# Attention, DFT mixing and feed-forward in one program: the feed-forward two slots earlier, w2's low halves on VectorE, the layer norm of even chunks in one block

## The chip, the cores and the metric

The kernel runs on one core of a Trainium2 chip. The metric is the device time of one execution in microseconds. The time before is the median of three runs. The trace is of one more execution, with the profiler on.

## What is computed

```python
# attention: local window of 32 keys each side plus 32 global tokens, 8 batches, 8 heads, 512 + 32 tokens, head 64
s_ll = where(|i - j| <= 32, q_l @ k_l.T / 8, -1e9);  s_lg = q_l @ k_g.T / 8
out_l = softmax([s_lg, s_ll]) @ [v_g; v_l];          out_g = softmax(q_g @ [k_g; k_l].T / 8) @ [v_g; v_l]
x = heads of [out_g; out_l] side by side             # (8, 544, 512)
# mixing and feed-forward
u  = x + real(fft(fft(x, axis=1), axis=2))
un = (u - mean(u)) / sqrt(var(u) + 1e-6)
y  = u + relu(un @ w_ch1) @ w_ch2                    # w_ch1 512 x 2048, w_ch2 2048 x 512
```

## The kernel before

All matrix products take fp16 operands in two parts, a high half and a low half (the value less its high half), and three matmuls for each product. So every operand is split: one copy to fp16 on ScalarE, one subtraction on GpSimd or VectorE. A DMA transpose on SyncE's queue turns what TensorE needs turned.

The work has three parts, which overlap:

- **Attention**, in slots. A batch takes 16 slots (four pairs of heads, four slots each, 128 queries a slot); six empty slots (`PAUSE`) stand after the first batch. A pair's scores go to one PSUM buffer of which there is a single copy (tag A): `scores` (L398) and the global queries' `g_scores` (L468) take turns in it. `masked` (L408, VectorE) and `exps` (L417, ScalarE) read the scores; `g_max` (L474 to L476, VectorE) and `g_exp` (L481, L482, ScalarE) read the global ones and so release the buffer for the next `scores`. `norm` is L457 to L459, `g_norm` L511 to L513, `scales` L315 to L332 (VectorE).
- **The DFT** of a batch, 8 to 21 slots after the batch's last slot R. `d_load` (R+8), `d_tail` on VectorE (L643 to L648, R+9.8), `d_even` on VectorE (L597, L599, R+10.4), `d_odd` on GpSimd (L593), then first and second products (L677, L707, from R+14), whose results are put together by `d_as` (L714, ScalarE) and `d_df` (L723, L724, VectorE) and added to x by `d_add` (L731, L732 on GpSimd, L733, L734 on VectorE) at R+17.6, R+18.6 and R+19.6. From the second batch on, the DFT's products use one PSUM bank, `bk1`.
- **The feed-forward**, in chunks of 256 rows, 17 of them: two for each batch, and one for the rest rows of all batches. A chunk has 16 steps, eight times a first product (`f_first`, L811, 24 matmuls), `f_hi` (L816, ScalarE), `f_lo` (L820, VectorE), and a second product (`f_second`, L830, 12 matmuls). `f_end` (L835) adds the result to u.

Ahead of a chunk stands its layer norm: `l_stats` (L760 to L763 on VectorE, L764 to L767 on GpSimd), and for each of two halves `l_un` (L774, L775, ScalarE), `l_lo` (L779, VectorE) and `l_turn` (L785, a transpose). `l_root` (GpSimd) is needed at the chunk's end only. The buffer `un` exists once, so the second `l_un` waits for the first `l_lo`. In `d_tail` the tile `st` has the same tag, so the same buffer.

The order on every engine is written by hand: `run` gives each call a time, and a sort by it makes one program order. Attention and DFT are given in slots (`add`), feed-forward and layer norm in steps (`at`). `warp` lays the slots onto the steps: up to `F0` = 37 they are the same, then 23 slots (16 + `PAUSE` + `LAG`) take the 32 steps of the first two chunks, and from then on each slot takes two steps. Engines run their own queue in order, as soon as what they wait for is there.

`w2` is split in `w_split(1, f)`, f = 0 to 15, one a slot from slot 33.75: `w_hi` (L252, ScalarE), a second ScalarE pass that scales the source in place (L261), a GpSimd subtraction (L262). `w1` is split the same way, but scaled by GpSimd (L259).

```python
        for c in range(17):
            F = F0 + 16 * c
            if c == 0:
                L, x, y, z = F - 4, (.50, .60), (.02, .06), (.30, .50)
            else:
                L, x, y, z = F - 6, (1.425, 2.425), (.335, .365), (.605, .605)
```

Of the kernel before, what the change touches and what calls it, by code (L numbers as in the profile page):

```python
# [8 lines left out]
F32 = mybir.dt.float32  # L9
# [4 lines left out]
AF = mybir.ActivationFunctionType  # L14
ALU = mybir.AluOpType
# [12 lines left out]
NVB = 2  # L28
NKB = 2
W0 = -8  # L30
F0 = 37
PAUSE = 6
LAG = 1
RS0 = 1.829591166069289e-20


# [39 lines left out]
class Plan:  # L76
# [3 lines left out]
    def add(self, slot, rank, fn, *a):  # L80
        self.at(self.warp(slot + rank), fn, *a)

    def at(self, time, fn, *a):
        self.q.append((time, len(self.q), fn, a))
# [6 lines left out]
class Kern:  # L91
# [163 lines left out]
    def w_split(self, k, i):  # L255
        nc = self.nc
        f, s, w = self.w_hi(k, i)
        if k == 0:
            nc.gpsimd.tensor_mul(f, f, s.to_broadcast([P, 512]))  # L259
        else:  # L260
            nc.scalar.activation(f, f, AF.Copy, scale=s)  # L261
        nc.gpsimd.tensor_sub(w[:, 1], f, w[:, 0])  # L262

    def b_load(self, b):
# [372 lines left out]

    def d_tail(self, b):
        ve, d = self.nc.vector, self.D[b]
        st = self.p1.tile([32, 256], F32, name="st", tag="un")  # L640
        et = d["et"] = self.p1.tile([32, 513], F32, name="et")
        xt = d["xt"]
        ve.tensor_sub(st[:, 1:256], xt[:, 1:256], xt[:, 511:256:-1])  # L643
        ve.tensor_add(xt[:, 1:256], xt[:, 1:256], xt[:, 511:256:-1])
        ve.tensor_add(et[:, 0:129], xt[:, 0:129], xt[:, 256:127:-1])
        ve.tensor_sub(et[:, 129:257], xt[:, 0:128], xt[:, 256:128:-1])
        ve.tensor_sub(et[:, 257:385], st[:, 1:129], st[:, 255:127:-1])
        ve.tensor_add(et[:, 385:513], st[:, 1:129], st[:, 255:127:-1])  # L648
# [197 lines left out]
    def run(self):  # L846
        self.h = {}
        late = F0 + 16 + PAUSE + LAG

        def warp(t):  # L850
            if t < F0:
                return t
            return F0 + 32 * (t - F0) / (16 + PAUSE + LAG) if t < late else F0 + 32 + 2 * (t - late)

        plan = Plan(warp)
        add, at = plan.add, plan.at
# [3 lines left out]
        for n in range(32):  # L860
            k, t = divmod(n, 16)
            i = t if k else 4 * (t % 4) + t // 4
            s = W0 + (n if k == 0 else 16 + 3 * t // 2)
# [3 lines left out]
            if n % 4 == 3 and k == 0:  # L867
                c = n // 4
# [6 lines left out]
        add(s + 1, .62, self.w_fold)  # L875
        add(s + 2, .62, self.w_scale, 1, 0)
        for f in range(16):
            add(s + 3 + f, .75, self.w_split, 1, f)
        add(8, .09, self.load_consts)

        for b in range(B):
# [49 lines left out]
        for b in range(B):  # L931
# [32 lines left out]
            add(t + 2, .07, self.d_rest, b)  # L964
        at(F0 + 32 * 7 + 4.5, self.l_load)
        for c in range(17):
            F = F0 + 16 * c
            if c == 0:
                L, x, y, z = F - 4, (.50, .60), (.02, .06), (.30, .50)
            else:  # L970
                L, x, y, z = F - 6, (1.425, 2.425), (.335, .365), (.605, .605)
            at(L + .42, self.l_stats, c)
            for j in range(2):
                at(L + x[j], self.l_un, c, j)
                at(L + x[j] + y[1], self.l_lo, c, j)
                at(L + x[j] + z[j], self.l_turn, c, j)
            at(L + 3.43, self.l_root, c)
            for fp in range(8):
                t = F + 2 * fp
                at(t + .30, self.f_first, c, fp)  # L980
                at(t + .97, self.f_hi, c, fp)
                at(t + 1.20, self.f_lo, c, fp)
                at(t + 3.30, self.f_second, c, fp)
            for j in range(2):
                at(F + 17.82, self.f_end, c, j)
            at(F + 18.04, self.f_out, c)
# [52 lines left out]
```

## Time and profile before

| what | us |
|---|---|
| median of 3 runs (1155.44 to 1157.02) | 1156.88 |
| the profiled execution's own time | 1152.42 |
| its span, first to last instruction | 1150.5 |
| TensorE busy | 962.0 |
| VectorE, ScalarE, GpSimd busy | 708.7, 633.6, 575.1 |
| first feed-forward matmul starts at | 220.4 |

The profile's page has the busy time of each engine, the span in 40 slices of 28.8 us, and the costliest groups. TensorE fills from the first feed-forward matmul on; ahead of it, the three other engines are the busy ones. All times in the rows are from the span's start.

### The profile page before, as it was taken

How to read it: one execution, taken by the hardware profiler on the slowest of the kernel's cores; microseconds unless marked ns; L12 is line 12 of the kernel's file. 1: busy time of each engine (PE TensorE's matmuls, PEld its weight loads, DVE VectorE, ACT ScalarE, POOL GpSimd, SP SyncE). 2: the span in 40 equal slices, each digit the busy share in tenths (PEclk: the TensorE clock that was granted, in tenths of full speed). 3: DMA queues.
4: the chain of work that ended last, by engine and by line, in shares of the span. 5: the costliest groups of instructions: out<-in, count | busy, mean ns of one | idle time of the engine just before them, and what ended most of it. 6: DMA issues, size and time to landing. Idle time of an engine off the chain costs nothing.

```text
span 1150.5 us, 25346 instructions
## 1 busy us (share of the span) xinstructions
PE 962.0 (84%) x9831; PEld 682.0 (59%) x9831; DVE 708.7 (62%) x1868; ACT 633.6 (55%) x1366; POOL 575.1 (50%) x728
## 2 busy tenths in 40 slices
PE   0244226588799899999999999999999999999996
PEld 0133215465576677676766676767677666666664
DVE  6997798547866865686568656866584444413211
ACT  5768558888676656665666566656564213212210
POOL 3789375778656554665465546654573312201100
PEclk9996557699899999999999999999999999999999
DMA  7578966567387465747465746573646212011100
GB/s 267 151 152 225 276 157 141 112 135 170 75 179 151 108 167 91 141 115 165 93 138 118 170 88 143 112 179 72 135 79 130 60 58 65 24 46 38 19 19 19
DMA packets 249569, 137.63 MB, mean 120 GB/s; under 512 B 200576, under 2 KB 223200, under 8 KB 249448
## 3 DMA queue, kind: packets, MB, share of 16 engines
q1 hardware_dynamic: 249448, 136.01, 51.2%
q8 instruction: 77, 1.26, 0.5%
q14 instruction: 44, 0.36, 0.1%
HBM read 65.10 MB, written 18.35 MB: 73 GB/s over the span
## 4 chain that ended last, share of the span: by engine, by line
PE 55%; DVE 24%; ACT 8%; DMA 6%; POOL 4%; issue 2%; SPq 0%; DVEq 0%; POOLq 0%; ACTq 0%
PE ps L811 22%; PE acc L830 22%; PE S L398 2%; DMA xt<-xs 2%; ACT pe L417 2%; DVE pe L408 2%; DMA qk<-in_qk 2%; PE bk L707 2%; DVE h L820 1%; PE S L468 1%; DVE ps L195 1%; DVE ps L196 1%; DVE z L328 1%; DVE wm L197 1%; DVE ps L194 1%
## 5 line engine op out<-in xcount | busy, mean ns | idle before, releaser
L811 PE MATMUL ps<-uh,wh 128*128 128x256 f16 x3264 | 383.4, 275 | 0.0
L830 PE MATMUL acc<-wh,h 128*128 128x512 f16 x1632 | 377.3, 381 | 4.1 <-DVE u L835 2.9
L811 PEld LDWEIGHTS <-wh 128*128 128x128 f16 x3264 | 319.2, 99 | 59.4 <-issue 0.7
L830 PEld LDWEIGHTS <-h 128*128 128x128 f16 x1632 | 153.5, 99 | 174.1 <-issue 9.2
L820 DVE SCALAR_TENSOR_TENSOR h<-ps,h 128x512 f16<-128x512 f32 x136 | 93.3, 686 | 188.6 <-ACT h L816 188.0
L425 POOL TENSOR_TENSOR ph<-pe,ph 128x448 f16<-128x448 f32 x128 | 137.2, 1072 | 143.0 <-ACT ph L421 88.5
L816 ACT ACTIVATE h<-ps 128x512 f16<-128x512 f32 x136 | 80.2, 589 | 223.4 <-PE ps L811 223.3
L417 ACT ACTIVATE pe<-pe,nm 128x224 f32<-128x224 f32 x256 | 102.0, 469 | 72.1 <-DVE nm L408 71.8
L408 DVE CUSTOM_DVE_ANT_0 pe<-S,msk,z 128x224 f32<-128x224 f32 x256 | 99.6, 445 | 7.5 <-PE S L398 3.6
L446 PE MATMUL bk<-vN,pl 128*128 128x65 f16 x768 | 72.9, 203 | 31.9 <-DMA pl<-ph 10.0
L398 PE MATMUL S<-kT,qT 64*128 64x192 f16 x768 | 55.7, 269 | 44.1 <-ACT pg L482 37.5
L398 PEld LDWEIGHTS <-qT 64*128 64x128 f16 x1536 | 53.7, 101 | 49.7 <-issue 38.9
L446 PEld LDWEIGHTS <-pl 128*128 128x128 f16 x768 | 62.2, 104 | 23.9 <-DMA pl<-ph 18.4
L421 ACT ACTIVATE ph<-pe 128x448 f16<-128x448 f32 x128 | 72.0, 562 | 0.0
L448 PEld LDWEIGHTS <-pl 96*128 96x128 f16 x768 | 60.1, 104 | 17.3 <-issue 10.5
L764 POOL TENSOR_SCALAR ve<-ve 128x2 f32<-128x2 f32 x17 | 5.8, 339 | 113.3 <-DVE ve L763 113.1
L376 POOL TENSOR_TENSOR kT<-qk,kT 128x512 f16<-128x512 f32 x32 | 40.7, 1272 | 36.4 <-ACT kT L371 33.0
L723 DVE SCALAR_TENSOR_TENSOR asm<-bk,dsc,asm 128x258 f32<-128x258 f32 (+1 forms) x21 | 10.1, 482 | 75.1 <-PE bk L707 60.5
L448 PE MATMUL bk<-vB,pl 96*128 96x65 f16 x576 | 55.2, 204 | 0.0
L774 ACT ACTIVATE un<-u,ve 128x512 f32<-128x512 f32 x34 | 27.6, 811 | 47.7 <-DVE unh L779 37.7
L361 ACT ACTIVATE qk<-qk,z 128x512 f32<-128x512 f32 x64 | 45.2, 708 | 10.7 <-DVE z L326 10.7
L262 POOL TENSOR_TENSOR wh<-wm,wh 128x512 f16<-128x512 f32 x32 | 38.0, 1188 | 19.7 <-ACT wm L261 18.3
(188 smaller groups left out, 1654.8 us busy)
## 6 DMA issues: line engine op xcount, KB each, us to landing
qk<-in_qk SPq DMA_DIRECT2D x32, 512.0 KB
vf<-in_v SPq DMA_DIRECT2D x32, 320.0 KB
raw<-in_moe_w_ch SPq DMA_DIRECT2D x18, 512.0 KB
xs<-x SPq DMA_DIRECT2D x32, 256.0 KB
out<-u SPq DMA_DIRECT2D x16, 512.0 KB
rw<-in_moe_w_ch SPq DMA_DIRECT2D x12, 512.0 KB
x<-xs SPq DMA_DIRECT2D x24, 256.0 KB
u<-xs SPq DMA_DIRECT2D x24, 256.0 KB
```

The lines of the kernel that those rows point to most:

```text
L361: self.nc.scalar.activation(s[nm], s[nm], AF.Copy, scale=s["z"][:, 3:4] if nm == "q" else s["z"][:, 4:5])
L398: nc.tensor.matmul(ps, qT[r, a, j], k, start=m == 0, stop=m == 2)
L408: nc.vector.tensor_tensor_reduce(self.per[(4 * p + j) % 4][:, h, 0:224], S[:, h, 224 * n:224 * n + 224], self.msk[:, j], z[:, 8:9], 3e38, ...
L417: nc.scalar.activation(pe[:, h, 0:224], pe[:, h, 0:224], AF.Exp, bias=nm[:, n, h:h + 1], scale=-1.0)
L421: self.nc.scalar.activation(ph[:, 0, :, 0:224], self.per[i % 4][:, :, 0:224], AF.Copy)
L425: self.nc.gpsimd.tensor_sub(ph[:, 1, :, 0:224], self.per[i % 4][:, :, 0:224], ph[:, 0, :, 0:224])
L446: nc.tensor.matmul(pv[:, j % 2, h], pl[:, 4 * a + 2 * h], vN[:, j, c, h, :], start=m == 0, stop=False)
L448: nc.tensor.matmul(pv[:, j % 2, h], pl[0:96, 4 * a + 2 * h + 1], vb, start=False, stop=m == 2)
L811: nc.tensor.matmul(ps[:, q], wt[:, w, c0:c0 + P], uh[:, :, 4 * a + kt, :], start=n == 0, stop=n == 11)
L816: self.nc.scalar.activation(h[:, 0], self.fps, AF.Relu)
L820: self.nc.vector.scalar_tensor_tensor(h[:, 1], self.fps, 0.0, h[:, 0], op0=ALU.max, op1=ALU.subtract)
L830: nc.tensor.matmul(self.acc_f[j], h[:, a, q, j * P:(j + 1) * P], self.w[1, f][:, w, :], start=f == 0 and a == 0 and w == 0, stop=f == 15 a ...
```

## The change

- `F0` is 35 instead of 37, and `LAG` 0 instead of 1: the feed-forward stands two slots earlier, and 22 slots instead of 23 lie over the first two chunks. After these the attention of a given slot stands beside steps that are six later (three slots) than before.
- `w_split` for w2: one VectorE instruction makes the low half from the unscaled source. The second ScalarE pass and the GpSimd subtraction go. The splits are given in steps, not slots, so they come one each step.
- `st` in `d_tail` has a buffer of its own.
- Layer norm: for the first chunk it begins 2.8 steps ahead instead of 4. For the even chunks 2 to 14, which are a batch's first, it begins 3.9 steps ahead instead of 6, and both halves follow each other directly. Odd chunks and the last are as they were in steps.

```diff
-F0 = 37
+F0 = 35
-LAG = 1
+LAG = 0
-            nc.scalar.activation(f, f, AF.Copy, scale=s)
+            nc.vector.scalar_tensor_tensor(w[:, 1], f, s, w[:, 0], op0=ALU.mult, op1=ALU.subtract)
+            return
         nc.gpsimd.tensor_sub(w[:, 1], f, w[:, 0])
-        st = self.p1.tile([32, 256], F32, name="st", tag="un")
+        st = self.p1.tile([32, 256], F32, name="st")
-            add(s + 3 + f, .75, self.w_split, 1, f)
+            at(s + 3 + f + .75, self.w_split, 1, f)
             if c == 0:
-                L, x, y, z = F - 4, (.50, .60), (.02, .06), (.30, .50)
+                L, x, y, z = F - 2.82, (.44, .50), (.02, .06), (.20, .30)
+            elif c % 2 == 0 and c < 16:
+                L, x, y, z = F - 3.9, (.50, .60), (.02, .06), (.30, .50)
```

Lines behind the added ones move by one: L643 of before is L644 of the change, and so on.

**VectorE, the tail of the fourth batch's DFT** (slots 79 and 80). `st`, `xt`, `et` are `d_tail`, `x_6575` is `d_even`, `h` is `f_lo`, `ng` is `g_max`. Before:

```order
L643 TENSOR_TENSOR st<-xt 32x255
L644 TENSOR_TENSOR xt<-xt 32x255
L645 TENSOR_TENSOR et<-xt 32x129
L646 TENSOR_TENSOR et<-xt 32x128
L647 TENSOR_TENSOR et<-st 32x128
L648 TENSOR_TENSOR et<-st 32x128
L597 TENSOR_TENSOR x_6575<-x_6575 128x4x255
L599 TENSOR_TENSOR x_6575<-x_6575 128x2x257
L820 SCALAR_TENSOR_TENSOR h<-ps_6794,h 128x512
L474 TENSOR_REDUCE ng<-S 64x1
```

And with the change:

```order
L645 TENSOR_TENSOR xt<-xt 32x255
L646 TENSOR_TENSOR et<-xt 32x129
L647 TENSOR_TENSOR et<-xt 32x128
L648 TENSOR_TENSOR et<-st 32x128
L649 TENSOR_TENSOR et<-st 32x128
L780 TENSOR_TENSOR unh<-un,unh 128x512 x2
L598 TENSOR_TENSOR x_6681<-x_6681 128x4x255
L600 TENSOR_TENSOR x_6681<-x_6681 128x2x257
L821 SCALAR_TENSOR_TENSOR h<-ps_6918,h 128x512
L475 TENSOR_REDUCE ng<-S 64x1
```

Both `l_lo` of the odd chunk 5 now stand between `d_tail` and `d_even`; before they stood two and a half slots later, behind `scales`.

**VectorE, the end of the third batch's DFT** (slot 71). `asm` and `u` are `d_df` and `d_add`, `nm` is the end of `masked`. Before:

```order
L408 ISA nm 128x1
L723 SCALAR_TENSOR_TENSOR asm<-bk_128,dsc,asm 128x2x129
L724 SCALAR_TENSOR_TENSOR asm<-bk_128,dsc,asm 128x2x129
L733 TENSOR_TENSOR u<-u,asm 128x257
L734 TENSOR_TENSOR u<-u,asm 128x255
L820 SCALAR_TENSOR_TENSOR h<-ps_5917,h 128x512
```

With the change:

```order
L409 ISA nm 128x1
L761 BN_STATS bst<-u 128x6
L762 BN_AGGR mv<-bst 128x2
L761 BN_STATS bst<-u 128x6
L762 BN_AGGR mv<-bst 128x2
L763 TENSOR_SCALAR ve<-mv 128x2
L764 TENSOR_SCALAR ve<-ve 128x2
L780 TENSOR_TENSOR unh<-un,unh 128x512 x2
L724 SCALAR_TENSOR_TENSOR asm<-bk_128,dsc,asm 128x2x129
L725 SCALAR_TENSOR_TENSOR asm<-bk_128,dsc,asm 128x2x129
```

The whole layer norm of the even chunk 4 now stands ahead of `d_df`, which empties `bk1`; before it stood two slots later, around `scales`.

**VectorE, ahead of the first feed-forward product** (slot 32). `wsc` is w2's scale, `dn` is the first row of `norm`. Before:

```order
L734 TENSOR_TENSOR u<-u,asm 128x255
L232 TENSOR_SCALAR wsc<-bk_128 128x1
L233 RECIPROCAL wsc<-wsc 128x1
L234 TENSOR_SCALAR wsc<-wsc 128x1
L236 TENSOR_SCALAR wsc<-wsc 128x4
L237 TENSOR_SCALAR wsc<-wsc 128x1
L457 TENSOR_SCALAR dn<-bk_127,z 128x4
```

With the change:

```order
L735 TENSOR_TENSOR u<-u,asm 128x255
L761 BN_STATS bst<-u 128x6
L762 BN_AGGR mv<-bst 128x2
L761 BN_STATS bst<-u 128x6
L762 BN_AGGR mv<-bst 128x2
L763 TENSOR_SCALAR ve<-mv 128x2
L764 TENSOR_SCALAR ve<-ve 128x2
L232 TENSOR_SCALAR wsc<-bk_128 128x1
L233 RECIPROCAL wsc<-wsc 128x1
```

The six statistics rows, which stood behind this slot's `norm` and `masked`, now follow `d_add` at once.

## Rows read from the trace of the kernel before

**Rows 1.** The page: busy tenths in 40 slices, and the clock.

```profile
PE   0244226588799899999999999999999999999996
PEclk9996557699899999999999999999999999999999
```

**Rows 2.** Windows: length, busy (instructions) of PE, PEld, DVE, ACT, POOL; clock, DMA.

```profile
209.40:220.40 11.00, 3.66 (x43) 2.65 (x44) 5.74 (x20) 9.55 (x21) 8.23 (x9) 0.50 0.98 200
220.40:291.90 71.50, 58.65 (x682) 42.29 (x680) 45.43 (x124) 62.09 (x133) 58.35 (x73) 0.93 0.60 133
291.90:360.00 68.10, 63.45 (x737) 45.31 (x735) 49.46 (x140) 49.54 (x112) 44.46 (x56) 0.98 0.61 123
476.50:591.70 115.20, 111.52 (x1193) 78.98 (x1192) 76.82 (x205) 71.31 (x160) 64.94 (x82) 0.99 0.57 131
```

**Rows 3.** Timeline: start, duration, engine, line, instruction [idle before <-releaser]; the start.

```profile
208.58 0.21 PE L446 MATMUL bk<-vN,pl 128*128 128x65 f16 x1 [2.73 <-DVE xg L513]
213.49 0.64 PE L468 MATMUL S<-kT,gT 128*64 128x512 f16 x1 [4.09 <-DVE nm L408]
220.37 1.89 PE L811 MATMUL ps<-uh,wh 128*128 128x256 f16 x8
```

**Rows 4.** Timeline: the DFT's add and the first chunk's layer norm.

```profile
196.96 0.74 POOL L732 TENSOR_TENSOR u<-u,asm 128x255 f32<-128x255 f32 x1
...
203.09 0.81 ACT L774 ACTIVATE un<-u,ve 128x512 f32<-128x512 f32 x1 [2.76 <-POOL ve L767]
```

**Rows 5.** Groups by line and shape: count, busy us, mean ns, idle before.

```profile
L774 ACT ACTIVATE un<-u,ve 128x512 f32<-128x512 f32 x34 | 27.6, 811 | 47.7 <-DVE unh L779 37.7 <-POOL ve L767 9.8
L775 ACT ACTIVATE unh<-un 128x512 f16<-128x512 f32 x34 | 21.4, 630 | 1.1
L261 ACT ACTIVATE wm<-wm,wsc 128x512 f32<-128x512 f32 x16 | 11.6, 722 | 0.5
L262 POOL TENSOR_TENSOR wh<-wm,wh 128x512 f16<-128x512 f32 x32 | 38.0, 1188 | 19.7 <-ACT wm L261 18.3
L636 DVE SCALAR_TENSOR_TENSOR eh<-s,dsc,eh 128x512 f16<-128x512 f32 x8 | 6.7, 840 | 0.0
```

**Rows 6.** Timeline: TensorE's waits around the second chunk, by three releasers.

```profile
307.23 1.02 PE L830 MATMUL acc<-wh,h 128*128 128x512 f16 x4 [2.86 <-DVE u L835]
352.00 0.19 PE L446 MATMUL bk<-vN,pl 128*128 128x65 f16 x1 [1.43 <-DVE xg L513]
```

**Rows 7.** Timeline: DVE, ACT and PE at the fourth batch's `d_tail`.

```profile
495.92 2.38 DVE L643 TENSOR_TENSOR st<-xt 32x255 f32<-32x255 f32 x1
504.43 0.26 DVE L476 TENSOR_SCALAR ng<-ng,z 64x1 f32<-64x1 f32 x1
505.82 0.42 PE L398 MATMUL S<-kT,qT 64*128 64x192 f16 x6 [0.28 <-ACT pg L482]
622.36 0.42 PE L398 MATMUL S<-kT,qT 64*128 64x192 f16 x6 [1.61 <-ACT pg L482]
```

**Rows 8.** Timeline: the third batch's second products at slot 71.

```profile
443.77 0.49 DVE L723 SCALAR_TENSOR_TENSOR asm<-bk,dsc,asm 128x258 f32<-128x258 f32 x1 [2.43 <-ACT qk L361]
447.52 0.34 PE L707 MATMUL bk<-c2r,z 128*18 128x129 f16 x3
```

**Rows 9.** Timeline: TensorE's waits beside layer norms and `scales`, and VectorE's longest of these.

```profile
465.88 0.19 PE L446 MATMUL bk<-vN,pl 128*128 128x65 f16 x1 [1.37 <-DVE xg L513]
526.93 0.34 PE L677 MATMUL bk<-c1r,eh 128*128 128x137 f16 x3 [2.03 <-DVE x L459]
756.33 0.34 PE L677 MATMUL bk<-c1r,eh 128*128 128x137 f16 x3 [1.94 <-DVE x L459]
809.37 0.19 PE L446 MATMUL bk<-vN,pl 128*128 128x65 f16 x1 [1.25 <-DVE xg L513]
462.42 2.13 DVE L328 SCALAR_TENSOR_TENSOR z<-z 128x2 f32<-128x2 f32 x1
```

**Rows 10.** One line's instructions: ns min/median/max; `scales` on VectorE.

```profile
L328 DVE SCALAR_TENSOR_TENSOR z<-z x16: 162/948/2131, 22.6 to 806.0; 128x2 f32<-128x2 f32 x16
```

## The prediction

> **What bounds the kernel now.** I read the slices of the page first. The reader is to see two regimes: up to the eighth slice TensorE is mostly idle and at varying clock, and from then on it is at 80 to 100% and, but for a few slices, at full clock [rows 1]. The windows say how full it is: in the first chunk TensorE is busy 58.65 of 71.50 us, in the second 63.45 of 68.10, in a later pair of chunks 111.52 of 115.20 [rows 2]. So from 220.4 us on the end is set by TensorE's work plus its idle time. All matmuls stay, at about the same clock, so the sum needs two things: when the first feed-forward matmul can start (and what attention work it pushes behind itself), and which of TensorE's waits go or come. In the first chunk ScalarE is as full as TensorE (62.09 of 71.50), GpSimd nearly (58.35), VectorE is not (45.43) [rows 2]. That matters for the w2 edit.
>
> **A, the start.** Of before, TensorE's last `values` ahead of slot 35.3, where the first product now stands, began at 208.58 and was done by about 209.4; then it sat idle 4.09 us up to 213.49. The first product came at 220.37 [rows 3]. From 209.4 to 220.4 TensorE was busy 3.66 of 11.00 us [rows 2]. That attention work now comes behind or between, so the most that can be won is 11.0 - 3.7 = 7.3 us. Against it stands the first chunk's layer norm, which moves up to right behind `d_add`. Its second statistics instruction reads what GpSimd's L732 leaves, at 196.96 + 0.74 = 197.7 [rows 4], while VectorE gets there at about 195.4; so VectorE waits 1.5 us or more there, and behind it wait this slot's scale, `norm` and `masked`. ScalarE's first L774, which was done after a wait of 2.76 us at 203.09 [rows 4], now waits from about 195.4 to about 200, and the second one waits for a `l_lo` that stands behind `masked`. This slot's `exps`, ahead of the layer norm before, stand behind it. Following both queues, the next slots come 3 to 5 us later and the first product at about 212, not 209.4. I take -(220.4 - 212) + 3.7 = **-4.7 us**; bounds -7.3 (the layer norm costs nothing) and 0 (the lateness passes on whole).
>
> **B, the first two chunks.** The w2 edit takes 722 ns from ScalarE and 1188 ns from GpSimd for each split, and gives VectorE one instruction of a form that is there already: L636, 128x512 from fp32 with a scalar, 840 ns [rows 5]. Fourteen splits stand behind slot 35, twelve of before behind slot 37. So ScalarE loses 12 x 0.72 = 8.6 us of the first chunk's work and VectorE gets 14 x 0.84 = 11.8 us: VectorE goes from 64% to 80% of the stretch, ScalarE from 87% to 75%. The low half moreover waits, in VectorE's queue, for ScalarE's high half, with `masked` and `f_lo` behind it; before, GpSimd did the waiting. I take nothing for the edit, bounds -8.6 and +11.8. Three waits of TensorE I count. The wait of 2.86 us for `f_end` (L835) goes [rows 6], since `f_end` no longer stands behind `scales`; but now it stands behind `d_tail`, and I give half back: -2.9 + 1.5. The wait of 1.43 us beside chunk 2's layer norm [rows 6] goes: -1.4. And chunk 2's new layer norm stands on ScalarE ahead of `d_as`, with its second half behind a `l_lo` that stands behind `masked`: on the two engines some 9.5 us of work lie between two of the DFT's products, under which TensorE has 5: +4.5 (bounds 0 and +4.5). Together **+1.7 us**.
>
> **C, odd chunks from the third batch on.** Between `d_tail` and `d_even` VectorE now has both `l_lo`. The first releases `un`, ScalarE then does L774 and L775 (0.81 + 0.63 us [rows 5]), and only then can the second go, so VectorE's chain grows by 0.69 + 1.44 + 0.69 = 2.8 us (0.69 is the usual `l_lo`). In the fourth batch that chain has no gap: it begins with L643 at 495.92, ends with `g_max` at 504.43, `g_exp` follows, and TensorE's `scores`, which need the PSUM buffer, wait at 505.82 already (0.28 us), in the fifth batch 1.61 us [rows 7]. What is late there is late on TensorE. Four batches (third to sixth) have next to no slack at this place: 4 x 2.8 - 0.3 = +10.9. The seventh has about 2.7 us of slack, the eighth no attention beside it: nothing. In exchange the waits at the old place go, where the layer norm and `scales` fell together: 2.03 us at 526.93 and two like it (the last 1.94 at 756.33 [rows 9]), with what hangs on them 6.0. **+4.9 us**; bounds -6 (the new place is covered) and +11 (the old waits stay, with `scales` alone).
>
> **D, even chunks.** At slot 71 the whole block stands ahead of `d_df`, which empties `bk1`. Of before, VectorE idled 2.43 us up to 443.77 and then did `d_df`; TensorE used the bank again at 447.52 [rows 8], about 2.9 us after it was free. The statistics (2.1 us) fit into that idle time. Then come 0.9 us on GpSimd, 1.4 on ScalarE, 0.7 on VectorE, 1.4, 0.7: `d_df` is done at about 449.5 instead of 444.7, and TensorE waits 2.0 us. Four batches: +8.0. The old waits beside even layer norms go, 1.37 us at 465.88 and three like it (the last 1.25 at 809.37 [rows 9]): -5.4. **+2.6 us**; bounds -5.4 and +8.
>
> **Nothing** for `st`'s own buffer (the same six instructions; it only keeps `l_un` from waiting for `d_tail`), for `l_root` (12 short GpSimd instructions, needed at the chunk's end) and for the later DFT of the last batch: it ends in chunk 14, and its layer norm begins some 13 us of TensorE work ahead of its product, for about 12 us of chain.
>
> **What the skill says.** VectorE's `scales` on 128x2 take 162 ns at best and 2131 at worst [rows 9, 10], the worst while GpSimd works. The Trainium skill (SBUF — State Buffer, section "SBUF: two separate sides") says that VectorE and GpSimd share a port pair as an exclusive lock, taken also by a VectorE instruction with two SBUF inputs against a GpSimd instruction that reads SBUF. The trace agrees with a wait of that kind. It speaks against this edit, since the new w2 instruction has two such inputs: by it each of the 14 could wait for a GpSimd instruction of some 1.2 us, 16.8 us in all, where L636's mean is only 0.1 us above its usual duration.
>
> **Sum.** Made against the profiled execution: 1152.4 - 4.7 + 1.7 + 4.9 + 2.6 = 1156.9, that is +4.5 us. The median of the runs is 4.5 us above that execution (1156.88 against 1152.42), so for the median I predict **1161.4**.
>
> **The rivals.** *ScalarE was the bound of the first chunk, and its relief shortens the slots* (faster). For it: 62.09 of 71.50 busy. Against: TensorE is as full, and VectorE takes over more than ScalarE gives. 12 x 0.72 = 8.6 off: 1152.8. It decides the sign if more than about half of it arrives. *The new stalls of C and D don't come*, since VectorE gets to these places earlier than I think (faster): 1161.4 - 10.9 - 8.0 = 1142.5. Against it: no gap on VectorE from L643 to `g_max`. *VectorE becomes the first chunk's bound* (slower): the splits wait on ScalarE and on GpSimd, 11.8 us on the path: 1173.2. For it: `masked` and `f_lo`, on which TensorE waits, stand in the same queue; against: 45.43 busy of 71.50 leaves room. *The change doesn't do what it says*: the early start is eaten by the early layer norm, A is 0: 1166.1.
>
> **How the numbers follow.** Forecast 0.42, first rival 0.22, second 0.13, third 0.15, fourth 0.08. The forecast's own spread is 1156 to 1167 (A and D at their ends). The range of 8 in 10 reaches from 1149 to 1172: it holds the first and fourth rival and most of the third, and leaves out the second and the far part of the third. 0.2% is 2.3 us, about what a measurement tells from no change. Faster: the second rival, two thirds of the first, a little of the forecast: 0.33. Same: a third of the first, a quarter of the forecast: 0.18. Slower: the rest, 0.49.
>
> **What would show it.** The first L811 at about 212 us (A). The pair of the first two chunks about as long as before, 71.5 + 68.1 = 139.6 us [rows 2], less the work of one slot that went over to later (B). TensorE waits of about 3 us before L398 (one line later) once a batch, released by `g_exp`, from the third batch on (C), and of 2 us before L707, released by `d_df` (D); none left beside `scales`. The forecast is wrong if the later pairs of chunks keep their 115.2 us or fall below, or if the first pair falls by more than 8 us.

## The result, and the profile after the change

| | us |
|---|---|
| before, median of 7 runs (1153.98 to 1159.13) | 1157.02 |
| after, median of 7 runs (1160.45 to 1163.49) | 1161.94 |
| ratio after to before, 95% interval | 1.0050 (1.0034 to 1.0066) |
| the profiled execution of after, and its span | 1161.94, 1160.2 |
| TensorE, VectorE, ScalarE, GpSimd busy | 969.0, 685.1, 623.7, 555.0 |
| first feed-forward product starts at | 209.4 |

The change makes the kernel 0.5% slower. The profiled execution of before was one of its quickest (1152.42 us; over all measurements its runs lie between 1151 and 1161), so the two traces differ by 9.7 us where the medians differ by 4.9. Differences below that come from traces are read with this in mind; those between runs are ratios to runs of before on the same chip, turned into us with 1157.

**Where the traces part.** The windows of after, in the columns of [rows 2]: first chunk, second chunk, and the pair of the fifth and sixth.

```profile
209.40:276.20 66.80, 58.28 (x650) 41.24 (x643) 49.08 (x141) 53.74 (x119) 45.08 (x62) 0.92 0.64 128
276.20:355.10 78.90, 64.93 (x732) 45.74 (x725) 51.66 (x131) 47.95 (x108) 40.58 (x40) 0.91 0.61 135
...
472.20:587.90 115.70, 111.55 (x1193) 79.22 (x1192) 70.03 (x207) 71.63 (x159) 64.10 (x83) 0.99 0.58 129
```

The reader is to see the lengths: the first chunk takes 66.8 us instead of 71.5, the second 78.9 instead of 68.1, a later pair 115.7 instead of 115.2 [rows 2]. Chunk 2 begins at 355.1 instead of 360.0. So the trace of after is 4.9 us ahead there, and from there to the end it needs 805.1 us where before needed 790.5. Of these 14.6 us, 5.7 are TensorE's waits. The view of TensorE's waits (releaser: us in total, times, longest) from chunk 2 on, first before, then after:

```profile
PE S L398 <- ACT pg L482: 5.5, 3, 3.6
PE bk L446 <- DVE xg L513: 5.4, 4, 1.4
PE bk L677 <- DVE x L459: 5.1, 3, 2.0
PE S L468 <- DVE nm L408: 0.9, 2, 0.4
```

```profile
PE bk L708 <- DVE asm L725: 12.6, 6, 2.3
PE acc L831 <- DVE u L836: 7.7, 4, 1.9
PE bk L447 <- DVE xg L514: 2.1, 3, 1.6
PE S L399 <- ACT pg L483: 0.2, 1, 0.2
```

The two lists have almost nothing in common: 16.9 us of old waits went (L398's are those of [rows 7], L446's and L677's those of [rows 9]), 22.6 us of others came. The rest, 8.8 us, is TensorE being busy longer: three more slots of attention stand behind chunk 2, and there are five stretches of 3.4 us at a granted clock of 1.2 GHz, each right behind a wait, against two before (the last microseconds, at 1.2 GHz in both, left out).

Most of the 14.6 us falls late. The windows of chunks 10 to 13 in the columns of [rows 2], first before, then after:

```profile
819.70:923.90 104.20, 104.20 (x1091) 73.89 (x1090) 58.67 (x157) 46.30 (x96) 48.03 (x65) 1.00 0.46 97
923.90:1013.30 89.40, 89.40 (x659) 60.93 (x657) 38.79 (x75) 21.31 (x36) 20.12 (x42) 1.00 0.18 50
```

```profile
816.80:928.10 111.30, 108.55 (x1135) 76.79 (x1134) 62.62 (x184) 53.85 (x112) 55.45 (x71) 0.98 0.46 97
928.10:1022.90 94.80, 92.52 (x712) 63.20 (x711) 38.62 (x83) 22.37 (x40) 19.81 (x41) 0.98 0.19 51
```

These four chunks take 206.1 us instead of 193.6, 12.5 more. Before, TensorE was busy there without a gap; now it has two waits for `d_df`, a stretch at 1.2 GHz behind each, and the attention of the three slots. Chunks 2 to 9 together take only 461.7 us instead of 459.7, since the new waits there stand in place of old ones.

**The first `L708` wait of the list (step D).** Timeline of VectorE and TensorE at the fourth batch's slot 87:

```profile
577.01 0.69 DVE L780 TENSOR_TENSOR unh<-un,unh 128x512 f16<-128x512 f32 x1 [1.55 <-ACT unh L776]
577.62 0.48 DVE L724 SCALAR_TENSOR_TENSOR asm<-bk,dsc,asm 128x258 f32<-128x258 f32 x1
...
578.55 0.33 PE L708 MATMUL bk<-c2r,z 128*18 128x129 f16 x3 [2.00 <-DVE asm L725]
```

VectorE waits 1.55 us for the second half's `un`, does `l_lo`, and only then `d_df`, for which TensorE waits 2.00 us.

**The `L831` waits.** Timeline of VectorE at the end of chunk 4, `f_lo`, `scales` (L316 to L333), `g_norm`, then `f_end`; and TensorE's wait:

```profile
530.13 0.69 DVE L821 SCALAR_TENSOR_TENSOR h<-ps,h 128x512 f16<-128x512 f32 x1
530.74 0.15 DVE L316 TENSOR_SCALAR z<-bk 128x6 int32<-128x6 int32 x1
...
531.73 1.24 DVE L319 TENSOR_SCALAR z<-z 128x4 int32<-128x4 int32 x1
533.00 1.14 DVE L329 SCALAR_TENSOR_TENSOR z<-z 128x2 f32<-128x2 f32 x1
534.06 1.07 DVE L330 TENSOR_SCALAR z<-z,ge 128x2 f32<-128x2 f32 x1
...
536.21 1.39 DVE L836 SCALAR_TENSOR_TENSOR u<-acc,ve,u 128x512 f32<-128x512 f32 x2
```

```profile
536.99 2.75 PE L831 MATMUL acc<-wh,h 128*128 128x512 f16 x12 [1.92 <-DVE u L836]
```

`scales` takes from 530.74 to 535.7, in instructions like the one of [rows 10] that can take 0.16 us; GpSimd works beside it without a gap from 530.65 to 535.1. In after it stands at the end of every chunk, right ahead of `f_end`; in before it stood six steps earlier. TensorE waits for `f_end` from 535.1 to 537.0. The four waits are those at the ends of chunks 2, 4, 6 and 8.

**The tail of the DFT (step C).** Timeline of after at the place of [rows 7], with GpSimd's `d_odd` (L594), and then the same in before (L593, and two of VectorE's):

```profile
508.76 2.35 POOL L594 TENSOR_TENSOR s<-x 128x1020 f32<-128x1020 f32 x1
...
511.56 0.41 DVE L644 TENSOR_TENSOR st<-xt 32x255 f32<-32x255 f32 x1
...
515.48 0.69 DVE L780 TENSOR_TENSOR unh<-un,unh 128x512 f16<-128x512 f32 x1 [1.55 <-ACT unh L776]
...
518.55 0.67 DVE L475 TENSOR_REDUCE ng<-S 64x1 f32<-64x512 f32 x1
```

```profile
495.68 2.34 POOL L593 TENSOR_TENSOR s<-x 128x1020 f32<-128x1020 f32 x1 [6.32 <-DMA x<-xs]
...
498.34 1.14 DVE L644 TENSOR_TENSOR xt<-xt 32x255 f32<-32x255 f32 x1
...
501.56 1.54 DVE L599 TENSOR_TENSOR x<-x 128x514 f32<-128x514 f32 x1
...
503.62 0.67 DVE L474 TENSOR_REDUCE ng<-S 64x1 f32<-64x512 f32 x1
```

Both `l_lo` are in the chain, with the idle 1.55 us that was forecast. Yet from `d_tail`'s first instruction to `g_max`'s first it takes 7.0 us, and before, with neither of them, 7.7 (495.92 [rows 7] to 503.62). Three of the chain's instructions took 2.38, 1.14 and 1.54 us in before and take 0.41, 0.41 and 0.70 in after, 3.5 us less: in before GpSimd's `d_odd` and what follows it ran beside them, in after `d_odd` is done when `d_tail` begins. 7.7 - 3.5 + 2.8 = 7.0. It is so in the other batches too: L643 takes 2.35, 2.38 and 2.35 us in the third to fifth batch of before, and its like L644 takes 0.40 to 0.41 us in the third to eighth of after.

**The start (step A).** Timeline of after, TensorE and VectorE:

```profile
209.45 3.28 PE L812 MATMUL ps<-uh,wh 128*128 128x256 f16 x24
...
219.13 0.64 PE L469 MATMUL S<-kT,gT 128*64 128x512 f16 x1 [4.38 <-DVE nm L409]
```

```profile
208.52 2.72 DVE L330 TENSOR_SCALAR z<-z,ge 128x2 f32<-128x2 f32 x1
```

The first product came 11.0 us earlier, and then the second only at 220.68: VectorE stood in `scales` (one instruction 2.72 us), then came a w2 split and `d_df` of the last tile, with `masked` behind them, and TensorE waited 4.38 us for that. Where before it waited ahead of the first product ([rows 3]: 4.09 us), it now waits behind it.

### The profile page after: what moved, and what is told of

It is laid out like the page before. It is cut to its first block, busy times and chain, and to the rows that moved or that the text cites. A ratio compares the mean times of both kernels' runs of the same rounds, so it can differ in the third digit from the quotient of the medians.

```text
span 1160.2 us, 25359 instructions
## 1 busy us (share of the span) xinstructions
PE 969.0 (84%) x9831; PEld 686.0 (59%) x9831; DVE 685.1 (59%) x1884; ACT 623.7 (54%) x1350; POOL 555.0 (48%) x712
## 4 chain that ended last, share of the span: by engine, by line
PE 54%; DVE 25%; ACT 8%; POOL 5%; issue 4%; DMA 3%; SPq 0%; DVEq 0%; POOLq 0%
PE ps L812 23%; PE acc L831 22%; DVE pe L409 2%; PE S L399 2%; DVE h L821 2%; ACT un L775 2%; DVE ps L195 1%; DVE ps L194 1%; ACT pe L418 1%; DVE ps L196 1%; PE bk L708 1%; PE bk L678 1%; DVE wm L197 1%; PE bk L447 1%; PE S L469 1%
## 5 line engine op out<-in xcount | busy, mean ns | idle before, releaser
L831 PE MATMUL acc<-wh,h 128*128 128x512 f16 x1632 | 378.2, 382 | 13.6 <-DVE u L836 13.6
L812 PE MATMUL ps<-uh,wh 128*128 128x256 f16 x3264 | 389.3, 277 | 0.0
L812 PEld LDWEIGHTS <-wh 128*128 128x128 f16 x3264 | 322.5, 100 | 63.0 <-issue 1.2
L831 PEld LDWEIGHTS <-h 128*128 128x128 f16 x1632 | 153.7, 99 | 184.6 <-issue 20.1
L449 PEld LDWEIGHTS <-pl 96*128 96x128 f16 x768 | 59.8, 104 | 12.5 <-DMA qk<-in_qk 5.3
L377 POOL TENSOR_TENSOR kT<-qk,kT 128x512 f16<-128x512 f32 x32 | 37.7, 1178 | 42.6 <-ACT kT L372 29.6
L780 DVE TENSOR_TENSOR unh<-un,unh 128x512 f16<-128x512 f32 x34 | 24.4, 719 | 41.4 <-ACT unh L776 41.4
L698 DVE SCALAR_TENSOR_TENSOR z<-bk,z 128x274 f16<-128x274 f32 x28 | 13.2, 472 | 58.3 <-ACT z L687 58.3
L732 POOL TENSOR_TENSOR u<-u,asm 128x257 f32<-128x257 f32 x16 | 13.3, 830 | 70.0 <-DVE asm L725 65.6
```

Of the source, the lines that this page charges most:

```text
L449: nc.tensor.matmul(pv[:, j % 2, h], pl[0:96, 4 * a + 2 * h + 1], vb, start=False, stop=m == 2)
L812: nc.tensor.matmul(ps[:, q], wt[:, w, c0:c0 + P], uh[:, :, 4 * a + kt, :], start=n == 0, stop=n == 11)
L831: nc.tensor.matmul(self.acc_f[j], h[:, a, q, j * P:(j + 1) * P], self.w[1, f][:, w, :], start=f == 0 and a == 0 and w == 0, stop=f == 15 a ...
```

## The experiments

All are the changed kernel, or the kernel before, with one edit. The number in brackets is the 95% interval of the ratio to before; after the change it is 1.0050.

**1. `even`: the even chunks' layer norm taken apart about `d_df`.** The seven numbers are steps from the chunk's start: statistics, then `l_un`, `l_lo`, `l_turn` of each half. `d_df` is at -2.88; without the edit all but the last turn stand ahead of it.

```diff
+SPLIT.update({c: (-3.48, -3.40, -2.87, -2.50, -2.865, -2.62, -2.30) for c in range(4, 16, 2)})
```

> The changed kernel with the layer norm of the even chunks 4 to 14 taken apart: statistics and the first L775/L776 stay ahead of d_df, both l_lo and the second L775/L776 go behind it. Theory (step D of the prediction, as the changed kernel's trace shows it): the whole layer norm ahead of d_df is what makes TensorE wait six times 2.0 to 2.3 us ahead of L708, and four of these waits are followed by 3.4 us at the granted clock of 1.2 GHz, some 1.7 us each. Without them: 6 x 2.1 + 4 x 1.7 = 19 us off, 1143; the lines that answer to the waits at 462.5, 576.6, 691.8, 807.1, 917.3 and 1012.5 are gone, and so are the low-clock stretches behind four of them. Rival (the wait only moves): TensorE waits as long, now for g_max behind the moved l_lo or for the first product of the next chunk: 1160 to 1164.

Measured: 1146.39 us, 0.9936 (0.9924 to 0.9948), 13.2 us less than after. TensorE's waits from chunk 2 on:

```profile
PE acc L833 <- DVE u L838: 7.7, 4, 1.9
PE bk L449 <- DVE xg L516: 4.6, 5, 1.6
```

All six waits for `d_df` are gone and no stretch at 1.2 GHz is left between 372 and 1139 us. The forecast was 19; some 2.5 us came back as waits for `g_norm` (2.1 to 4.6 us), and the traces differ by 15.5. D's mechanism is shown, and the rival, that the wait only moves, is out.

**2. `scales`: `scales` behind `f_end`.**

```diff
-                add(G - 5, .62, self.scales, p // 2)
+                add(G - 5, .92 if G > 61 else .62, self.scales, p // 2)
```

> The changed kernel with scales (from the third chunk on) put behind f_end instead of ahead of it. Theory: the changed LAG put scales, whose 128x2 instructions take 1.1 to 1.2 us each beside GpSimd, right ahead of f_end, and this is the wait of 1.9 us ahead of L831 in every even chunk's end (four of them). Without it 4 x 1.9 = 7.6 us off: 1154. Rival: f_end is late for d_lo and d_tail_lo ahead of it, or scales, now later, delays the next L362 and with it the attention: under 2 us off, 1160 to 1163.

Measured: 1151.74 us, 0.9967 (0.9953 to 0.9982), 9.6 us less than after. In the same view:

```profile
PE bk L708 <- DVE asm L725: 12.5, 6, 2.3
PE bk L244 <- DVE xg L514: 1.9, 4, 0.5
```

The four waits for `f_end` are gone, and so is the 1.6 us beside `g_norm`. So `scales` ahead of `f_end` cost them, not `d_lo` or `d_tail_lo`.

**3. `both`: the two edits together.**

> The changed kernel with both edits that gained, the even layer norms taken apart about d_df and scales behind f_end. The two remove different waits in different chunks. Theory: the gains add, 13.2 + 9.6 = 22.8 us off the changed kernel's 1161.9: 1139, ratio to before 0.985. Rival (with one wait gone the other's neighbour becomes late): less than 17 us, 1145 and up.

Measured: 1134.19 us, 0.9819 (0.9798 to 0.9839), 26.7 us less than after: the gains add (22.8 us by the two alone, a difference at the edge of the intervals). From chunk 2 on TensorE waits 2.1 us in all, and the trace needs 776.3 us there instead of 805.1. That fall of 28.8 us is what the list and the clock say: 20.5 us of waits and five stretches of 3.4 us at half the clock, 8.5 us. From chunk 2 on the cause is therefore shown: beside the attention that came there, the change lost by two things, the layer norm ahead of `d_df` and `scales` ahead of `f_end`, and by what they did to the clock.

**4. and 5. The second chunk's two long waits, one at a time.** `ln2` moves chunk 2's `l_un` behind `d_as` and its second `l_lo` behind `d_df`; `tail` moves the second batch's `d_tail` behind `f_end`.

```diff
+SPLIT[2] = (-3.38, -3.02, -2.795, -2.65, -2.75, -2.07, -1.95)
```

```diff
-            add(R + 9, .80, self.d_tail, b)
+            add(R + 9, 1.265 if b == 1 else .80, self.d_tail, b)
```

> The changed kernel with chunk 2's layer norm alone taken apart: L775/L776 behind d_as, the second l_lo behind d_df. Theory (step B, its third wait): the wait of 6.07 us ahead of L708 at 337.6 is chunk 2's layer norm ahead of d_as, with its second half behind masked. Without it 6.1 us and about 2 us of low clock behind it go: 1154 to 1156. Rival: the first two chunks are bound by another engine's work, so that TensorE waits elsewhere instead: 1160 to 1163.

> The changed kernel with the second batch's d_tail put behind f_end of the first chunk. Theory: the wait of 5.93 us ahead of L831 at 286.7 is f_end behind d_tail, which first waits for its DMA (2.18 us) and then runs beside GpSimd (L644 2.11 us where it takes 0.41 alone). Without it 5.9 us and some 2 us of low clock go: 1154 to 1156. Rival: d_tail, now later, delays d_even and g_max behind it, and TensorE waits there: 1160 to 1163.

Measured: `ln2` 1159.30 us, 1.0041 (1.0029 to 1.0053), within its interval of after; `tail` 1160.06 us, 1.0053 (1.0041 to 1.0064), no change. Both rivals hold. The timeline of TensorE shows where the wait went, first in `ln2`, where L710 is the changed kernel's L708 and L717 `d_as` of the last tile, then in `tail`, where L483 is `g_exp`:

```profile
349.54 0.81 PE L710 MATMUL bk<-c2r,z 128*18 128x129 f16 x6 [4.53 <-ACT asm L717]
```

```profile
297.39 0.66 PE L399 MATMUL S<-kT,qT 64*128 64x192 f16 x6 [5.50 <-ACT pg L483]
```

In `tail` the moved `d_tail` takes as long as it did (L644 2.24 us, beside GpSimd), now ahead of `g_max`.

**6. and 7. `all2` and `best`: these two moved further.** In `all2` `d_tail` goes behind `g_max` (1.695 for 1.265), and chunk 2's layer norm wholly behind `d_df`; in `best` its first `l_un` goes forward to where ScalarE is free. Both keep the two edits of `both`.

```diff
-SPLIT[2] = (-2.075, -1.565, -1.235, -1.02, -1.025, -0.795, -0.60)
+SPLIT[2] = (-3.38, -2.59, -2.075, -1.9, -1.565, -1.5, -1.46)
```

> As the run before it, and chunk 2's layer norm wholly behind d_df (first L775 behind the last d_as, second behind f_hi), and the second batch's d_tail behind g_max of its slot. Theory: the two waits of 6.07 and 5.93 us in the second chunk only moved in the last two experiments because what was moved stood ahead of another operation TensorE waits for (the last d_as; g_exp); behind those, both go, some 10 us with their stretches at 1.2 GHz: 1129. Rival: the first two chunks are bound by VectorE's and ScalarE's chains, and the waits move once more: 1137 to 1140.

> As all2, with chunk 2's layer norm earlier: statistics behind masked, first L775 behind p_hi, first l_lo behind d_df, second L775 behind the last d_as. Theory: the 5.48 us that TensorE waited ahead of chunk 2's first product in all2 were its late second DMA transpose, and go, with some 2 us at 1.2 GHz; nothing waits in exchange, since ScalarE's queue is never held ahead of d_as: 1125 to 1128. Rival: ScalarE held by the second L775, or VectorE by l_lo ahead of g_max, gives the wait back: 1131 to 1134.

Measured: `all2` 1132.50 us, 0.9804 (0.9783 to 0.9825); `best` 1129.12 us, 0.9765 (0.9738 to 0.9792). `all2` lies between its theory and its rival, `best` 1 us above its theory. `all2` won less than 2 us on `both`: its first pair of chunks fell from 146.6 to 142.0 us, but TensorE then waited 5.48 us for chunk 2's transposes, too late now. In `best` that wait is gone, and a wait of 3.01 us for the last `d_as` came. What still bounds the first two chunks there stays open. So `best` is 27 us faster than before and 33 faster than after, and in its later pairs TensorE is busy for 109.75 of 110.40 us:

```profile
351.00:461.40 110.40, 109.75 (x1192) 78.19 (x1193) 68.08 (x208) 71.23 (x159) 64.96 (x83) 1.00 0.60 136
```

**8. `w2old`: the changed kernel without the w2 edit.**

```diff
-            nc.vector.scalar_tensor_tensor(w[:, 1], f, s, w[:, 0], op0=ALU.mult, op1=ALU.subtract)
-            return
+            nc.scalar.activation(f, f, AF.Copy, scale=s)
```

> The changed kernel with w2's low halves made as before, by a second ScalarE pass and a GpSimd subtraction. Theory (step B): the edit is worth nothing, 1160 to 1164, the first product and the first two chunks' 66.8 and 78.9 us as they are. First rival (ScalarE was the bound): 14 splits x 0.72 us come back on ScalarE, the first chunk 5 to 9 us longer, 1167 to 1171. Third rival (VectorE's new 14 x 0.84 us are on the path): the first chunk shorter, 1150 to 1156.

Measured: 1172.62 us, 1.0157 (1.0138 to 1.0177), 12.4 us more than after (10.7 by the medians alone). The first rival holds: the first chunk takes 76.1 us, as against 66.8, the pair 157.5 as against 145.7. The timeline of `w2old`, TensorE and ScalarE:

```profile
248.89 0.66 PE L398 MATMUL S<-kT,qT 64*128 64x192 f16 x6 [3.70 <-ACT pg L482]
```

```profile
244.20 0.72 ACT L261 ACTIVATE wm<-wm,wsc 128x512 f32<-128x512 f32 x1
...
247.34 0.58 ACT L816 ACTIVATE h<-ps 128x512 f16<-128x512 f32 x1
247.81 0.76 ACT L481 ACTIVATE pg<-S,ng,z 64x512 f32<-64x512 f32 x1
```

ScalarE works without a gap from 237.6 on, `g_exp` stands at its end, and TensorE waits 3.70 us for it; `g_max` had been done at 243.2. In the first chunk TensorE's waits for `g_exp` come to 6.4 us, in after to 1.6: that is 4.8 of the 9.3 us. TensorE is also busy 3.2 us longer there, at a mean clock of 0.86 against 0.92.

**9. `w2before`: the kernel before with the w2 edit alone.** The diff is that of experiment 8, the other way round.

> The kernel before with the w2 edit alone. Theory (from undoing the edit in the changed kernel, which cost 10.7 us): ScalarE's second pass bounds the first chunk in the kernel before as well (62.09 of 71.50 us busy), so the first pair of chunks gets 8 to 11 us shorter: 1145 to 1149, ratio 0.99 to 0.993. Rival: with the start at slot 37 twelve splits stand behind it and only some of them late, TensorE waits for w2 but 0.9 us there; 1153 to 1157.

Measured: 1148.94 us, 0.9935 (0.9911 to 0.9959), 7.5 us less than before. By time it is the theory. But its profiled execution, 1152.82 us, was its slowest, no shorter than the one of before, and shows only 2.3 us in the first pair of chunks (137.3), so where the 7.5 us come from is not shown.

**10. and 11. `start` and `startw2`: the early start alone, without and with the w2 edit.** The first chunk's layer norm and the splits move with it as in the change. `LAG` 3 puts chunk 2 and all behind it against the same slots as before.

```diff
-F0 = 37
+F0 = 35
-LAG = 1
+LAG = 3
-            add(s + 3 + f, .75, self.w_split, 1, f)
+            at(s + 3 + f + .75, self.w_split, 1, f)
-                L, x, y, z = F - 4, (.50, .60), (.02, .06), (.30, .50)
+                L, x, y, z = F - 2.82, (.44, .50), (.02, .06), (.20, .30)
```

> The kernel before with the early start alone: F0 = 35 with LAG = 3, so that from chunk 2 on every operation stands against the attention as before, the first chunk's layer norm behind d_add as in the changed kernel, and w2's splits timed by the feed-forward's own steps as there, but made as before. Theory (step A): the first product at about 209 to 210 us, 11 us earlier, the two first chunks longer by two slots of attention work, some 7.3 us (3.66 us each by the prediction's window): -3.7, 1151 to 1153, ratio 0.9965. Rival (the early layer norm and the denser w2 splits eat it): within 2 us of before.

> The early start alone (F0 = 35, LAG = 3, the run before) with the w2 edit. Theory: the first two chunks advance by the attention's slots, about 6.1 us each whatever feed-forward lies beside them, so an early start gives nothing by itself and its cost (9.3 us) stays: with the edit some 10 us less than the early start alone, 1153 to 1156, and slower than the edit alone. Rival (the early start only lost because ScalarE was full): with the edit it pays the 3.7 us forecast for it, 1142 to 1145 if the edit alone gives 1147.

Measured: `start` 1164.86 us, 1.0090 (1.0070 to 1.0109); `startw2` 1165.45 us, 1.0064 (1.0039 to 1.0089). The early start costs 10 us without the edit, and 15 with it (against `w2before`); for `startw2` neither the theory nor the rival came. (The expectation of `start` counts 3.66 us for each of two slots; the window of [rows 2] has 3.66 for both together.) The first product came at 209.5, and chunk 2, which begins in the same slot as before, at 370.0 instead of 360.0. The waits of `start` in its first pair of chunks:

```profile
PE S L398 <- ACT pg L482: 6.2, 4, 3.7
PE S L468 <- DVE nm L408: 4.8, 2, 4.4
PE bk L446 <- DVE xg L513: 4.8, 2, 3.4
PE ps L811 <- DMA uh<-unh: 4.4, 1, 4.4
PE acc L830 <- DVE h L820: 2.7, 1, 2.7
```

These are many waits, for VectorE, for ScalarE and for a transfer, and no one of them is as long as the loss. From the first product to chunk 2 `start` takes 160.5 us; before took 150.6 for the same slots, from 209.4 on. TensorE idles 4.2 us more in it, and is busy 5.7 us longer. Per slot the pair takes 6.4 us (160.5 for 25 slots), before 6.1 (139.6 for 23), after 6.6 (145.7 for 22), `w2old` 7.2. That a slot of attention has a length of its own here, whatever feed-forward lies beside it, as the theory of `startw2` has it, is not shown by these. Which wait of `start` carries the 10 us, and why the edit gains nothing on top of it (160.4 against 160.5 us in the traces), stays open.

**12. `oddlate`: `d_odd` behind `p_lo`.**

```diff
-            add(R + 10, .355, self.d_odd, b)
+            add(R + 10, .365, self.d_odd, b)
```

> The changed kernel with d_odd, GpSimd's first large step of the DFT, put behind p_lo instead of ahead of it in every batch. Theory of why step C's stall did not come: VectorE's chain from d_tail to g_max takes 7.0 us in the changed kernel, though both l_lo stand in it, against 8.5 us before, because GpSimd's L594 is now done before d_tail begins and L644 takes 0.41 instead of 2.38 us; the chain ends only some 0.5 us ahead of TensorE's need. With d_odd some 6 us later d_even waits for it, the chain gets 1 to 3 us longer, and TensorE waits ahead of L399 for g_exp in the third to sixth batch, 4 to 10 us in all: 1166 to 1172. Rival: there is slack enough, and the order of d_odd is worth nothing: 1160 to 1164.

Measured: 1175.76 us, 1.0160 (1.0133 to 1.0187), 12.7 us more than after, and above the theory's range. Timeline of VectorE, and the waits of TensorE from chunk 2 on:

```profile
520.56 2.22 DVE L780 TENSOR_TENSOR unh<-un,unh 128x512 f16<-128x512 f32 x1 [1.54 <-ACT unh L776]
```

```profile
PE bk L708 <- DVE asm L725: 12.5, 6, 2.3
PE acc L831 <- DVE u L836: 10.8, 4, 2.7
PE S L399 <- ACT pg L483: 4.3, 5, 0.9
```

GpSimd's `d_odd` now runs beside the second `l_lo`, which takes 2.22 instead of 0.69 us; the chain to `g_max` is 1.5 us longer, and the waits for `g_exp` that step C forecast are there, 4.3 us in five. (The 8.5 us that the expectation gives for before run to `g_max`'s last instruction; to its first it is 7.7.) The theory's mechanism holds, but the larger part of the time went elsewhere: the waits for `f_end` grew from 1.9 to 2.7 us, and with each of them now goes a stretch of 3.4 us at 1.2 GHz.

## Why the prediction came out as it did

The forecast, 1161.4 us, is within 0.6 of the median. Three of its four steps failed, and that the sum held is luck.

**A, the start, -4.7: the step failed.** The first product came even earlier than forecast (209.4, not 212). But the step took the idle time ahead of it for time to be won. `start` and `startw2` show that an earlier start, with what moves along with it, costs 10 to 15 us. The waits stand in the attention's own chain and are met again behind the product (4.09 us ahead of it in before, 4.38 us behind it in after). The 3.7 us of attention that A counted as pushed back were also overpriced: that window of [rows 2] has a clock of 0.50, and from chunk 2 on three more slots cost TensorE about 8.8 - 3 x 1.7 = 3.7 us together.

**B, the w2 edit, nothing: the step failed.** It is worth 12.4 us in the changed kernel and, by the runs, 7.5 in the one before; the first rival (8.6 us) had it, and had 0.22. On top of the early start alone it showed no clear gain. The argument against it, that TensorE was as full as ScalarE and VectorE took over more than ScalarE gave, compared busy shares over a chunk, while what `w2old` shows as the largest loss is the wait for one instruction, `g_exp`, at the end of ScalarE's queue. The third rival's premise, that the splits would wait for ScalarE and hold VectorE up, is partly there (VectorE waited 10.1 us for `wh` in six places), but the edit gained all the same. From the Trainium skill's rule on the shared port pair (SBUF — State Buffer, section "SBUF: two separate sides") the prediction had estimated a loss of up to 16.8 us. The trace has 2.4: the sixteen new instructions take 752 ns in the median and 1677 at most, 2.4 us more than sixteen of the usual 0.74. It agrees with the rule, but not with that price. Seven take 808 ns or more; each of them began while a GpSimd instruction was under way, and none lost more than what was left of that one. Of the three waits that B listed, that of chunk 2's layer norm came (6.07 us, forecast 4.5), and that for `f_end` was 5.93 us where 1.5 was left to it, since the second batch's `d_tail` waited 2.18 us for its DMA and then ran beside GpSimd (L644 2.11 us). A and B together: chunk 2 began 4.9 us earlier in the traces, where the two terms, without the work pushed back, add up to 6.7.

**C, odd chunks, +4.9: the step failed.** The lengthening by the two `l_lo` is there, the waits that go are gone, but the waits that were to come are 0.2 us instead of 11. C added its 2.8 us to a chain measured in before, of which 3.5 us went with where GpSimd's work lies and did not come along. `oddlate` puts some of the overlap back, and the waits appear. The Trainium skill's rule on the port pair (SBUF — State Buffer, section "SBUF: two separate sides") would have been worth asking here rather than at the w2 edit, since an instruction like L643 has two SBUF inputs. The traces agree with a wait of that kind: 2.38 us beside L593, 0.41 without it. In place of the waits that C forecast came four waits of 1.9 us for `f_end`, which the prediction did not see: it followed the layer norms to their new places against the attention, but not `scales`, which moved by the same six steps.

**D, even chunks, +2.6: right in the mechanism and in the size of a wait, not in their number.** Each wait is 2.0 us, as worked out, and `even` shows the cause. The step missed two of six: in the seventh and eighth batch it expected nothing, yet there the layer norm and `d_df` alone make 2.3 and 2.3 us. And it left out the clock, 1.7 us behind most of these waits.

**The sum.** Between the traces, which the terms were read from, the change costs 9.7 us, where the sum has 4.5. The medians differ by 4.9 because the profiled execution of before was 4.6 us quicker than its median. From chunk 2 on C and D were forecast at +7.5 us; TensorE's waits grew by 5.7, and the clock took another 3 x 1.7 = 5.1. The prediction lacked 19.5 us there (`f_end` 7.7, more waits for `d_df` 4.6, the clock 5.1, waits for `g_norm` 2.1) and had 16.2 too much: 10.7 of C's stalls, and 5.5 us of waits for `g_exp` that it let stand and that went. A's overpaid start is about B's unpaid edit. By a sign that it named itself, later pairs that keep their 115.2 us, the forecast was nearly wrong: that pair took 115.7. The second rival, that C's and D's stalls don't come, was half true, and would have been so entirely with the edits of `both`. No run takes back `st`'s own buffer by itself, so that it is worth nothing is not shown.

## What to carry to other kernels

When a schedule is shifted against another, list every instruction group that changes neighbours, not those alone that the change names: here `scales` moved by six steps, unnamed, and cost 9.6 us, where the layer norm that the change names cost 13.2. A chain's length measured beside a busy GpSimd holds only while that neighbour stays where it is; take the duration alone, and ask what runs beside it after the move. Idle time of TensorE in a stretch where other engines set the pace need not be there to be won by starting TensorE's work earlier: here that lost 10 to 15 us. First find the last link of the chain it waits for, which a busy share does not show.

## What the runs showed of the hardware

A wait of TensorE can cost more than its length. The windows of after, right behind two equal waits of 2.0 us for `d_df`:

```profile
579.10:582.50 3.40, 3.40 (x19) 2.30 (x18) 2.16 (x5) 2.38 (x8) 3.40 (x4) 0.50 0.78 145
464.60:468.00 3.40, 3.40 (x33) 2.64 (x32) 2.62 (x6) 2.38 (x7) 3.40 (x4) 1.00 0.82 154
```

In the first the granted clock is 0.50, 1.2 GHz, in the second 1.00, 2.4 GHz, though TensorE ran the same instructions in the same order for 20 us ahead of either wait. It fell behind four of the six waits for `d_df`, in `oddlate` at all four of 2.7 us for `f_end`. In after it also fell behind one of 1.61 us, but behind none of the four of 1.92 us, so the length of a wait alone doesn't decide. In the long stretches of `both` and `best` without such waits it never fell, up to the last microseconds. What decides, these runs don't show.
